# The last output block in two column halves, two late stores on another queue, one relu on another engine

## The chip, the cores and the metric

The kernel runs on one core of one Trainium2 chip. The metric is the time of one execution on the device, in microseconds (us). It is given as the median of several runs; one further execution was taken with the hardware profiler, and all views shown here come from such executions.

## The reference

The input `x` has 8 batches of 3072 rows and 256 columns. Each column is filtered along the rows by a Fourier transform, and the 24576 filtered rows then go through a small network:

```python
X = np.fft.rfft(x, axis=1)
y = np.fft.irfft(X * (filt_r + 1j * filt_i)[None], n=3072, axis=1)
t = y.reshape(24576, 256)
out = np.maximum(t @ w1, t @ w2) @ w_out      # w1, w2: 256 x 1024, w_out: 1024 x 256
```

## The kernel before

The Fourier transforms are done as matmuls with tables of sines, in stages with transposes through DRAM between them. The network is rewritten with max(a, b) = b + relu(a - b): `Wd` holds w1 - w2, `Wo` holds w_out, and `M` holds the product of w2 and w_out. So an output row is relu(t Wd) Wo + t M.

The rows are worked on in 64 tiles of 384 rows, numbered tt (eight for each batch). A tile's filtered rows lie in `yt[tt]`, its hidden values in `gt[tt]`. The loop at the end of the kernel runs over tt. In round tt it computes the hidden values of tile tt, in eight steps j of 128 hidden units (`moe_h`), and between these steps the output of tile tt - 1 (`moe_o`). A 65th round has only output matmuls left. The work of the next batch's Fourier stages is put between the steps by plans written out by hand; in the last batches little or nothing of it is left. The order of each engine's instructions is the order of the code.

In `moe_h`, step j makes one PSUM tile `ph` (L452 to L454), and relu moves it into `gt`. The table `on_v` and, from tile 8 on, the rule `j in (1, 3, 6)` say which steps VectorE does (L456); ScalarE does the others (L458).

In `moe_o`, an output tile is three blocks of 128 rows by 256 columns. Each block is a sum of ten matmuls (two with `M`, L484; eight with `Wo`, L486). Blocks are numbered q = 3 tt + c, from 0 to 191. Two blocks share one PSUM bank, and VectorE copies both at once into `ot` (L499). The last two blocks are copied on their own: block 190 by ScalarE (L490); block 191, which has a bank of its own, in two parts, columns 0 to 111 by ScalarE (L492) and columns 112 to 255 by VectorE (L493).

`out_block` issues the store of a block, 128 KB, to DRAM (L467). GpSimd issues it, but for the last two tiles (blocks 186 to 191), which SyncE issues. Each of these queues works in order: a store that waits for its copy holds up what is behind it. The pool `ps` has six PSUM buffers and `pso` has two; together they fill the eight banks.

Of the kernel before, what the change touches and what calls it, by code (L numbers as in the profile page):

```python
# [8 lines left out]
FP32 = mybir.dt.float32  # L9
BF16 = mybir.dt.bfloat16  # L10
AF = mybir.ActivationFunctionType
OP = mybir.AluOpType

B = 8
N = 3072
D = 256
# [10 lines left out]
def kernel(  # L27
# [14 lines left out]
    nc = tc.nc  # L42
    V, S, G, TE = nc.vector, nc.scalar, nc.gpsimd, nc.tensor
# [9 lines left out]
    Wo = const.tile([128, 8, D], BF16)  # L53
    M = const.tile([128, 2, D], BF16)
# [13 lines left out]
    ps = ctx.enter_context(tc.tile_pool(name="ps", bufs=6, space=bass.MemoryType.PSUM))  # L68
# [315 lines left out]

    def product(E, v, s, px, pool=None):
        pq = (pool or pqpool).tile([128, 2, 2, D], BF16, tag="pq", name="pq")
        E.tensor_tensor(pq, px.rearrange("p (o i) d -> p o i d", o=1).to_broadcast([128, 2, 2, D]),  # L387
                        F[:, :, 2 * v:2 * v + 2, s], OP.mult)
        return pq
# [36 lines left out]
    yt = {}  # L426

    def s4(tt):
        b, i = divmod(tt, 8)
        y_ = ypool.tile([128, 2, 384], BF16, tag="yt", name="y_")  # L430
        for dc in range(2):
# [11 lines left out]
    gt = {}  # L443
    on_v = {(i, j) for i in range(8) for j in range(8)
            if (j in (1, 4, 6) if 2 < 8 * i + j < 11 else j in (1, 2, 4, 6, 7) if 8 * i + j < 22
                else (j in (1, 5) and (i, j) != (3, 1)) or (i, j) == (3, 0) if 8 * i + j < 48 else j in (1, 3, 6))}

    def moe_h(tt, j):
        if j == 0:
            gt[tt] = gpool.tile([128, 8, 384], BF16, tag="gt", name="gt")  # L450
        y_ = yt[tt]
        ph = ps.tile([128, 384], FP32, tag="ps", name="ph")  # L452
        for dc in range(2):
            TE.matmul(ph, Wd[:, dc, 128 * j:128 * j + 128], y_[:, dc], start=(dc == 0), stop=(dc == 1))  # L454
        if (tt, j) in on_v if tt < 8 else j in (1, 3, 6):
            V.tensor_scalar(gt[tt][:, j], ph, 0.0, None, OP.max)  # L456
        else:
            S.activation(gt[tt][:, j], ph, AF.Relu)  # L458

    po = {}  # L460
    ot = {}

    def out_block(tt, c):
        b, i = divmod(tt, 8)
        dst = out[b * N:(b + 1) * N].rearrange("(c p i m) d -> c i p (m d)", c=3, p=32, i=8)[c, i]
        E = G if tt < 8 * B - 2 else nc.sync
        E.dma_start(out=dst, in_=ot[tt // 2][:, 3 * (tt % 2) + c])  # L467


    FIRST = ([(c, e) for c in (0, 2) for e in range(8)] + [(c, e) for c in (0, 2) for e in (8, 9)]  # L470
             + [(1, e) for e in range(10)])

    def moe_o(tt, k0, k1):
        y_, g_ = yt[tt], gt[tt]
        for k in range(k0, k1):
            c, e = divmod(k, 10) if tt else FIRST[k]
            n = e if tt else (e + 2) % 10
            q = 3 * tt + c
            blk = slice(128 * c, 128 * c + 128)
            if e == 0 and (q % 2 == 0 or q == 24 * B - 1):  # L480
                po[q // 2 % 2] = pso.tile([128, 2, D], FP32, tag="po", name="po")
            p_ = po[q // 2 % 2][:, q % 2]
            if n < 2:
                TE.matmul(p_, y_[:, n, blk], M[:, n], start=(e == 0), stop=(e == 9))  # L484
            else:
                TE.matmul(p_, g_[:, n - 2, blk], Wo[:, n - 2], start=(e == 0), stop=(e == 9))  # L486
            if e == 9 and q >= 24 * B - 2:
                e = q % 6
                if q % 2 == 0:
                    S.activation(ot[tt // 2][:, e], p_, AF.Copy)  # L490
                else:
                    S.activation(ot[tt // 2][:, e, 0:112], p_[:, 0:112], AF.Copy)  # L492
                    V.tensor_copy(ot[tt // 2][:, e, 112:D], p_[:, 112:D])  # L493
                out_block(tt, c)
            elif e == 9 and q % 2 == 1:
                if q % 6 == 1:
                    ot[tt // 2] = opool.tile([128, 6, D], FP32, tag="ot", name="ot")
                e = q % 6
                V.tensor_copy(ot[tt // 2][:, e - 1:e + 1], po[q // 2 % 2])  # L499
                for qq in (q - 1, q):  # L500
                    out_block(qq // 3, qq % 3)
# [206 lines left out]
    for tt in range(8 * B + 1):  # L708
        b, i = divmod(tt, 8)
        k = 0  # L710
        for j in range(8):
            step = 8 * i + j
            if tt < 8 * B:
                moe_h(tt, j)
            for fn, a in mid.get((b, step), ()):
                fn(*a)
            if tt > 0:
                n = 3 if j in (3, 7) else 4
                moe_o(tt - 1, k, k + n)
                k += n  # L720
            for fn, a in todo.get((b, step), ()):
                fn(*a)
            if j == (6 if i == 7 else 5 if tt == 3 else 4) and tt + 1 < 8 * B:
                s4(tt + 1)
# [30 lines left out]
```

## Time and profile before

| | |
|---|---|
| median of three runs | 501.27 us (500.65 to 502.88) |
| the profiled execution, its own time | 501.44 us |
| its span in the trace | 499.7 us |
| TensorE busy | 485.9 us (97%) |
| VectorE, ScalarE, GpSimd busy | 329.4, 309.5, 258.7 us |
| mean granted TensorE clock | 0.99 |
| last matmul ends | 494.7 us |
| last copy ends | 495.3 us |
| last store issued | 495.3 us |
| last instruction ends | 499.7 us |

Times inside the trace count from the start of its span. PE is TensorE, PEld its weight loads, DVE VectorE, ACT ScalarE, POOL GpSimd and SP SyncE; a q behind the name means its instruction queue, where stores are issued. In a line of the timeline the first number is the start, the second the length, and the bracket is the idle time of the engine before it and what ended that. The chain that ended last is followed back from the last instruction to what released it, step by step. DMA queue q1 carries what SyncE issues, q0 what GpSimd issues, and the queues called instruction carry the engines' code.

### The profile page before, as it was taken

How to read it: one execution, taken by the hardware profiler on the slowest of the kernel's cores; microseconds unless marked ns; L12 is line 12 of the kernel's file. 1: busy time of each engine (PE TensorE's matmuls, PEld its weight loads, DVE VectorE, ACT ScalarE, POOL GpSimd, SP SyncE). 2: the span in 40 equal slices, each digit the busy share in tenths (PEclk: the TensorE clock that was granted, in tenths of full speed). 3: DMA queues.
4: the chain of work that ended last, by engine and by line, in shares of the span. 5: the costliest groups of instructions: out<-in, count | busy, mean ns of one | idle time of the engine just before them, and what ended most of it. 6: DMA issues, size and time to landing. Idle time of an engine off the chain costs nothing.

```text
span 499.7 us, 13074 instructions
## 1 busy us (share of the span) xinstructions
PE 485.9 (97%) x5300; PEld 360.7 (72%) x5300; DVE 329.4 (66%) x514; ACT 309.5 (62%) x631; POOL 258.7 (52%) x342
## 2 busy tenths in 40 slices
PE   7689999999999999999999999999999999999995
PEld 3447777777777777777777777777777777777774
DVE  7876787558765678457865678457765588555552
ACT  5777488657774577647775578646776455544442
POOL 8794569339545683529446584439642211222220
PEclk9889999999999999999999999999999999999998
DMA  8999799997789668896589767895678525411112
GB/s 126 163 246 188 245 253 284 257 276 214 217 239 261 179 207 232 246 250 197 180 247 249 216 201 189 267 257 176 201 201 205 152 93 161 163 65 64 64 64 85
DMA packets 78046, 97.23 MB, mean 195 GB/s; under 512 B 8065, under 2 KB 54434, under 8 KB 77954
## 3 DMA queue, kind: packets, MB, share of 16 engines
q1 hardware_dynamic: 64786, 66.80, 50.4%
q0 software_dynamic: 13200, 29.60, 20.6%
q8 instruction: 41, 0.67, 0.6%
q14 instruction: 19, 0.16, 0.1%
HBM read 53.87 MB, written 47.19 MB: 202 GB/s over the span
## 4 chain that ended last, share of the span: by engine, by line
PE 94%; ACT 2%; DMA 2%; POOL 1%; issue 1%; DVE 0%; POOLq 0%
PE po L486 35%; PE ph L454 33%; PE po L484 8%; PE pz L405 5%; PE py L434 4%; PE px L381 2%; PE pa L354 2%; DMA xb<-in_x_dram 2%; PE pt L539 1%; PE pr L560 1%; POOL xb L88 1%; PE pa L329 1%; PE pt L533 1%; ACT bt L525 0%; PE pm__1147 L311 0%
## 5 line engine op out<-in xcount | busy, mean ns | idle before, releaser
L486 PE MATMUL po<-Wo,gt 128*128 128x256 bf16 x1536 | 261.1, 273 | 0.0
L458 ACT ACTIVATE gt<-ph 128x384 bf16<-128x384 f32 x321 | 157.8, 496 | 145.7 <-PE ph L454 144.8
L486 PEld LDWEIGHTS <-gt 128*128 128x128 bf16 x1536 | 145.9, 98 | 66.7 <-issue 12.0
L467 POOL DMA_DIRECT2D out_dram<-ot x186 | 102.9, 558 | 171.1 <-DVE ot L499 166.7
L456 DVE TENSOR_SCALAR gt<-ph 128x384 bf16<-128x384 f32 x191 | 104.5, 553 | 64.3 <-PE ph L454 60.7
L387 DVE TENSOR_TENSOR pq<-px,F 128x1024 bf16<-128x1024 f32 x91 | 106.9, 1218 | 26.2 <-PE px L381 25.9
L454 PEld LDWEIGHTS <-Wd 128*128 128x128 bf16 x1024 | 96.5, 98 | 12.5 <-issue 0.6
L103 POOL TENSOR_TENSOR xb<-XF 128x512 bf16<-128x512 f32 x48 | 61.3, 1276 | 51.4 <-DMA XF<-in_x_dram 40.4
L499 DVE COPY ot<-po 128x512 f32<-128x512 f32 x95 | 65.1, 685 | 24.8 <-PE po L486 24.8
L104 POOL TENSOR_TENSOR xb<-XF 128x512 bf16<-128x512 f32 x48 | 61.0, 1272 | 0.0
L358 ACT ACTIVATE at<-pa 128x512 bf16<-128x512 f32 x96 | 51.8, 611 | 4.2 <-PE pa L354 4.2
L409 ACT ACTIVATE zt<-pz 128x512 bf16<-128x512 f32 x84 | 45.6, 594 | 5.1 <-PE pz L405 0.8
L434 PE MATMUL py<-G,zr 96*128 96x96 bf16 x512 | 32.6, 206 | 0.1
L434 PEld LDWEIGHTS <-zr 96*128 96x128 bf16 x512 | 28.9, 97 | 2.4 <-DVE zr L563 0.6
L405 PE MATMUL pz<-pq,VP 64*64 64x256 bf16 x336 | 22.0, 281 | 0.0
L381 PE MATMUL px<-bt,U 64*64 64x256 bf16 x384 | 19.9, 278 | 1.2 <-ACT VQ L278 0.7
L405 PE MATMUL pz<-pq,VQ 64*64 64x256 bf16 x336 | 21.0, 269 | 0.0
L405 PEld LDWEIGHTS <-VP 64*64 64x64 bf16 x336 | 9.9, 105 | 13.3 <-issue 13.0
L354 PE MATMUL pa<-xb,CT 64*64 64x512 bf16 x192 | 17.6, 376 | 0.0
L381 PEld LDWEIGHTS <-U 64*64 64x64 bf16 x384 | 10.4, 108 | 3.9 <-issue 3.6
L570 PE MATMUL pd<-W 128*128 128x512 bf16 x28 | 9.7, 458 | 1.8 <-DVE zero L149 1.5
L405 PEld LDWEIGHTS <-VQ 64*64 64x64 bf16 x336 | 10.0, 106 | 0.0
(427 smaller groups left out, 603.4 us busy)
## 6 DMA issues: line engine op xcount, KB each, us to landing
out_dram<-ot POOLq DMA_DIRECT2D x186, 128.0 KB, 3.7
XF<-in_x_dram SPq DMA_DIRECT2D x96, 192.0 KB, 4.9
ad<-at SPq DMA_DIRECT2D x56, 192.0 KB, 3.7
zd<-zt SPq DMA_DIRECT2D x42, 256.0 KB, 2.8
zr<-zd SPq DMA_DIRECT2D x56, 192.0 KB, 4.8
bt<-ad SPq DMA_DIRECT2D x13, 768.0 KB, 10.7
WS<-in_moe_w_dram SPq DMA_DIRECT2D x4, 512.0 KB, 8.2
xb<-in_x_dram POOLq DMA_DIRECT2D x8, 192.0 KB, 6.2
```

What stands on the lines that cost most here:

```text
L103: G.tensor_tensor(t_[:, 0], f[:, 0], f[:, 1], OP.add)
L104: G.tensor_tensor(t_[:, 1], f[:, 0], f[:, 1], OP.subtract)
L358: S.activation(at[:, m0:m0 + 2], pa[g], AF.Copy)
L387: E.tensor_tensor(pq, px.rearrange("p (o i) d -> p o i d", o=1).to_broadcast([128, 2, 2, D]), F[:, :, 2 * v:2 * v + 2, s], OP.mult)
L405: TE.matmul(pz[g][64 * s:64 * s + 64, i], tab[64 * g:64 * g + 64, 2 * v + i, s], pq[s][64 * g:64 * g + 64, q, i], start=(q == 0), stop=(q ...
L434: TE.matmul(py[:, m], zr[b][:, 4 * i + m, 128 * dc:128 * dc + 128], G1, start=True, stop=True)
L454: TE.matmul(ph, Wd[:, dc, 128 * j:128 * j + 128], y_[:, dc], start=(dc == 0), stop=(dc == 1))
L456: V.tensor_scalar(gt[tt][:, j], ph, 0.0, None, OP.max)
L458: S.activation(gt[tt][:, j], ph, AF.Relu)
L467: E.dma_start(out=dst, in_=ot[tt // 2][:, 3 * (tt % 2) + c])
L486: TE.matmul(p_, g_[:, n - 2, blk], Wo[:, n - 2], start=(e == 0), stop=(e == 9))
L499: V.tensor_copy(ot[tt // 2][:, e - 1:e + 1], po[q // 2 % 2])
```

## The change

Block 191 is computed in two halves of 128 columns, by ten matmuls each, the first in the bank it had and the second in a tile `pl` of the pool `ps`. ScalarE copies the first half, VectorE the second. Stores 186 and 187 are issued by GpSimd instead of SyncE. The relu of tile 60, step 5, is done by VectorE instead of ScalarE.

```diff
-        if (tt, j) in on_v if tt < 8 else j in (1, 3, 6):
+        if (tt, j) in on_v if tt < 8 else j in (1, 3, 6) or (tt, j) == (8 * B - 4, 5):
             V.tensor_scalar(gt[tt][:, j], ph, 0.0, None, OP.max)
...
-        E = G if tt < 8 * B - 2 else nc.sync
+        E = G if 3 * tt + c < 24 * B - 4 else nc.sync
...
+    def last_block(tt, c, p_):
+
+        blk = slice(128 * c, 128 * c + 128)
+        for h, pp in enumerate((p_, ps.tile([128, 128], FP32, tag="ps", name="pl"))):
+            dd = slice(128 * h, 128 * h + 128)
+            for n in range(10):
+                l_, r_ = (yt[tt][:, n, blk], M[:, n, dd]) if n < 2 else (gt[tt][:, n - 2, blk], Wo[:, n - 2, dd])
+                TE.matmul(pp, l_, r_, start=(n == 0), stop=(n == 9))
+            if h == 0:
+                S.activation(ot[tt // 2][:, 3 * (tt % 2) + c, dd], pp, AF.Copy)
+            else:
+                V.tensor_copy(ot[tt // 2][:, 3 * (tt % 2) + c, dd], pp)
+        out_block(tt, c)
...
+            if q == 24 * B - 1:
+                if e == 9:
+                    last_block(tt, c, p_[:, 0:128])
+                continue
...
-            if e == 9 and q >= 24 * B - 2:
-                e = q % 6
-                if q % 2 == 0:
-                    S.activation(ot[tt // 2][:, e], p_, AF.Copy)
-                else:
-                    S.activation(ot[tt // 2][:, e, 0:112], p_[:, 0:112], AF.Copy)
-                    V.tensor_copy(ot[tt // 2][:, e, 112:D], p_[:, 112:D])
+            if e == 9 and q == 24 * B - 2:
+                S.activation(ot[tt // 2][:, q % 6], p_, AF.Copy)
                 out_block(tt, c)
```

## The prediction

> **What bounds the kernel now.** I read the page first: busy time by engine and the chain that ended last.
>
> ```profile
> PE 485.9 (97%) x5300; PEld 360.7 (72%) x5300; DVE 329.4 (66%) x514; ACT 309.5 (62%) x631; POOL 258.7 (52%) x342
> ...
> PE 94%; ACT 2%; DMA 2%; POOL 1%; issue 1%; DVE 0%; POOLq 0%
> ```
>
> TensorE carries 94% of the chain, and the change takes no arithmetic from it. So the edit can only act where TensorE is not the chain: behind its last matmul. I read that stretch next, in the chain of waits from 492.4 us to the end (start, length, what).
>
> ```profile
> 493.57 0.22 PE po L484 x2
> 493.79 0.89 PE po L486 x8
> 494.67 0.02 issue
> 494.70 0.27 ACT ot L492
> 494.97 0.02 issue
> 494.99 0.31 DVE ot L493
> ```
>
> The last block's ten matmuls take 1.11 us (0.22 + 0.89). Then ScalarE and VectorE copy their parts one after the other, although they touch different columns: 0.63 us from the last matmul to 495.30. The timeline from 494.5 us adds the store queue, SyncE (SPq):
>
> ```profile
> 494.52 1.35 SPq L467 DMA_DIRECT2D out_dram<-ot  x2
> 494.70 0.26 ACT L492 ACTIVATE ot<-po 128x112 f32<-128x112 f32 x1 [0.71 <-PE po L486]
> 494.99 0.31 DVE L493 COPY ot<-po 128x144 f32<-128x144 f32 x1 [1.79 <-ACT ot L492]
> ```
>
> The two issues under the first line lie at 494.52 to 495.06 (block 190, whose data was ready at 493.99 and waited for SyncE) and at 495.33 to 495.87 (block 191, the last). The last view is that of the stores themselves: how long each took from issue to landing (block 190 above, block 191 below), and what else the DMA engines carried from 496.8 to 497.4 us.
>
> ```profile
> DMA to landing us min/median/max: 2.0/2.0/2.0
> ...
> DMA to landing us min/median/max: 3.1/3.1/3.1
> ```
> ```profile
> q1 hardware_dynamic: 54, 0.04, 20.9%
> q14 instruction: 1, 0.01, 4.5%
> ```
>
> The last store needed 3.06 us (495.33 to 498.38) where the three before it needed 2.05 to 2.12. One packet of 8 KB of instructions starts at 496.86, amid its packets, and holds one DMA engine for 0.43 us (4.5% of 16 x 0.6 us). That engine's share of the store, eight packets, comes only after it, from 497.29 to 497.91; the other fifteen were done by 497.0. So about 1.0 us of the span is a collision of the last store with a load of code. Behind the landing are 1.3 us of closing semaphores, which the change does not touch.
>
> **The change, part by part.** The profiled execution took 501.44 us, 1.77 more than its span of 499.67; it lies 0.17 above the median of 501.27. I work out differences in the execution and apply them to the median.
>
> *Half-width matmuls.* Ten of 256 columns go, twenty of 128 come, each with its own weight load. The nearest row has this shape, 128x128 weights and 128 columns, from 42.29 us in the chain:
>
> ```profile
> 42.29 0.45 PE pt L304 x8
> ```
>
> That is 0.056 us each, so 20 x 0.056 = 1.12 against 1.11: TensorE ends at 494.68, 0.01 later. These are transposes, and a plain matmul could be slower; the upper bound is the duration of one weight load, 0.098 us (the page's weight-load rows), which gives 1.96. The lower bound is 20 x 0.043 = 0.86, from the L434 matmuls of 96 columns. I take 0.056, because its shape is the same and its weight loads, 0.098 us each, evidently overlap there.
>
> The Trainium skill, "TensorE: Matmul & The Clock Gate", section "Back-to-back issue gap", says that in a stream of weight loads and matmuls the spacing is set by both, and gives about 81 ns at 128 columns: by it the block would take 1.62 us. The row of this trace disagrees.
>
> *The copies.* Columns 0 to 127 are finished after ten half matmuls, at about 494.1; ScalarE's copy (0.264 us at 112 columns, 0.384 at 256, so 0.28) is over by 494.5 under the second half. VectorE copies the other 128 columns from another buffer: 309 ns at 144 columns and 692 at 512 give 1.04 ns a column, so 0.29 us. If it still waits for ScalarE through the tile `ot`, that wait is already over. It runs from 494.71 to 495.00 instead of ending at 495.30: 0.30 us saved.
>
> *What is late next: SyncE.* It is busy with block 190 until 495.06. Between two of its issues that wait on data stand 0.10 us (494.42 to 494.52). So block 191 cannot be issued before 495.16, and of the 0.30 only 0.17 remains.
>
> *Two stores to GpSimd.* Blocks 186 and 187 leave SyncE, where they were issued from 490.40 to 491.68. SyncE then waited for data until 493.23, so the removal starts nothing earlier. GpSimd's last work ended at 487.6; it issues both by about 491.5 (0.55 each, the page's L467 row), and they land some 2 us later, long before the end. Nothing is queued behind them. Their cover is 4.8 us (493.5 to 498.3); cost 0.
>
> *The relu.* Tile 60, j = 5 ran on ScalarE from 471.26 to 471.75. VectorE is free from 471.48 (its scaled copy L440) to 472.02, so the relu there takes 0.55 of a gap of 0.54 and pushes the next one by some 0.03. Its reader, the output matmul of the next tile, comes over 2 us later, and TensorE has no idle time there. Cost 0; without that cover it would be 0.06 (0.553 against 0.496).
>
> *The code load.* Which engine asked for it the trace does not say. Instruction counts fit VectorE: its 703 records at that moment are 128 more than the 575 at its load before, at 398.39. VectorE has one instruction more now, so the load should come a little earlier, as the store does. If the load stays at 496.86, the store, 0.17 earlier, has its packets done by 496.84 and all of 1.0 is gained. If it moves with the store, 0 is gained. If it moves 0.2 to 0.6 further ahead, the eight late packets follow it earlier and part is gained. Ends 0 and 1.0; I take 0.33, nearer to the lower end, because both events hang on the end of the same copy.
>
> The Trainium skill, "Runtime: NRT & Kernel Launch", section "Instruction fetch mechanics", calls the cost of crossing such a block mostly hidden; by it this term would be 0. The 3.1 against 2.0 above says that here it is not hidden.
>
> Sum: 0.17 + 0.33 = 0.5 us less; 501.27 - 0.5 = 500.8.
>
> **Rivals.**
>
> *Only the issue gain.* The load keeps hitting the last store in full: 501.27 - 0.17 = 501.1. For it: both move together. Against it: VectorE's extra instruction.
>
> *The load clears the store.* 0.17 + 1.0 less: 500.1. For it: 0.02 us are enough if the load stays in place, and an asked-for load that no longer hangs on the last copy would come microseconds earlier. Against it: nothing fixes its time.
>
> *Weight loads set the pace: slower.* At 0.098 us, the last matmul starts 19 x 0.098 = 1.86 us after the first (493.40), ends 0.22 later at 495.48, and VectorE is done at 495.81; the store is issued at 495.84, 0.51 late: 501.8. It decides from 0.071 us a matmul, where the copy ends at 495.30 as now. Only L304's 0.056 and L434's 0.043 speak against it. At the 81 ns of the Trainium skill ("TensorE: Matmul & The Clock Gate", "Back-to-back issue gap") the same sum gives an issue 0.19 late: 501.5.
>
> *A second code load: slower.* TensorE's own loads are larger: 41 of 16 KB on queue q8, the last at 481.38, and one fills a DMA engine for 0.96 us. They come some 250 TensorE records apart; 227 are left after the last one, and twenty more make 247. If one more falls into the last store, its 0.96 in place of 0.43 makes the store 0.5 later: 501.27 - 0.17 + 0.5 = 501.6; behind the other load on the same engine it would be 502.6.
>
> **How the numbers follow.** Forecast 0.45; only the issue gain 0.2; the load clears 0.15; weight loads 0.07; second load 0.1; 0.03 for what the trace does not show. The three runs spread from 0.6 below the median to 1.6 above. The low end is 500.1 less 0.3 of that spread, 499.8; the high end is 501.6 with 0.4, 502.0. What a measurement can tell from no change is about 0.5%, 2.5 us; no case reaches it, so nearly all lies within: 0.90. Faster by over 0.5% gets 0.06 and slower 0.04, for the remainder.
>
> **What would show it.** Right: twenty 128-column matmuls about 0.056 us apart; a single VectorE copy of 0.29 us after the last one; SyncE's last issue at about 0.17 us earlier and directly behind block 190; stores 186 and 187 on GpSimd, landed by 494. Wrong: a spacing of 0.07 or more, a last issue later than 495.33, a packet of q8 after 494, or a last store that lands in 2.05 us or in more than 3.1. A shift of the whole span ahead of 490 us would mean that I missed the mechanism.

## The result, and the profile after

The change makes the kernel slower: 503.69 us (median of 16 runs, 502.74 to 506.23) against 501.44 (16 runs). The ratio is 1.0042, with a 95% interval of 1.0029 to 1.0056: a loss of 0.4%. The profiled execution took 503.2 us, with a span of 501.4, 1.76 more than before.

The page answers to that of before line by line:

```profile
PE 485.5 (97%) x5307; PEld 361.2 (72%) x5310; DVE 329.7 (66%) x515; ACT 308.7 (62%) x630; POOL 259.6 (52%) x344
...
PE 91%; DMA 3%; DVE 2%; POOL 1%; issue 1%; ACT 0%; DVEq 0%; SPq 0%; POOLq 0%
```

TensorE is as busy as it was, and nothing here is 1.8 us longer. (Its share of the chain is lower by an early stretch in which the chain was followed through transfers instead; the last hidden matmul, L454, starts 0.26 us earlier than before, at 490.47.) The arithmetic at the end does what was said of it. The chain of waits of the changed kernel, from 493 us to the end (start, length, what):

```profile
493.31 0.56 PE po L480 x10
493.87 0.57 PE pl L480 x10
494.44 0.02 issue
494.47 0.29 DVE ot L484
```

Twenty half matmuls take 1.13 us, and one copy of 0.29 us follows instead of two in a row. The timeline from 494.2 us on has the store queue beside it:

```profile
493.65 1.89 SPq L467 DMA_DIRECT2D out_dram<-ot  x3
493.99 0.44 PE L480 MATMUL pl<-Wo,gt 128*128 128x128 bf16 x5
...
494.47 0.29 DVE L484 COPY ot<-pl 128x128 f32<-128x128 f32 x1 [1.52 <-PE pl L480]
```

VectorE no longer waits for ScalarE, and SyncE's three issues follow each other without a pause for data. The chain as the profile draws it ends here, at 494.76; the span ends at 501.4. No engine's counted work stands between. What lies there must be read elsewhere. First the last stores, from issue to landing:

```profile
DMA to landing us min/median/max: 2.0/2.1/2.1
```

(The line covers the last two stores.) The last one is issued at 495.00 and lands at 497.05, after 2.05 us instead of 3.06. So the stores too are done earlier than before. From 494 us on the DMA engines carry nothing but stores; the code packet is gone:

```profile
q1 hardware_dynamic: 576, 0.52, 18.8%
issues: line engine op xcount, KB each, median us to landing
out_dram<-ot SPq DMA_DIRECT2D x3, 128.0 KB, 2.1
```

The waits of SyncE's queue from 494 us on show the rest (who, for whom, us in total, times, longest):

```profile
SPq L763 <- PEq L763: 4.1, 2, 3.6
SPq L763 <- DMA out_dram<-ot: 1.0, 2, 0.6
```

and before:

```profile
SPq L750 <- DMA out_dram<-ot: 2.4, 2, 1.8
SPq L750 <- PEq L750: 0.7, 2, 0.5
```

The first line of after has grown from 0.7 to 4.1 us, the second has shrunk from 2.4 to 1.0. SyncE waits once for 3.6 us in the closing part of the program (L763 is the launch line, where the end of the kernel is booked). TensorE is named, but its own closing drain had ended at 494.48, so it cannot be what SyncE waited for. What the launch line's instructions did on each engine shows who was late. GpSimd (POOLq) has three closing DRAIN instructions there. After (duration in ns, min/median/max, then first and last start):

```profile
L763 POOLq DRAIN  x3: 51/106/9800, 490.8 to 501.2; - x3
```

and before, where the launch line is L750:

```profile
L750 POOLq DRAIN  x3: 51/106/9640, 487.0 to 499.4; - x3
```

The first of them is GpSimd's first closing instruction, and it lasts 9.64 us before and 9.80 us after. It stands right behind GpSimd's last store and ends 9.0 to 9.1 us after that store's issue ends. Before, it ran from 486.96 to 496.60, and SyncE's own closing drains were through at 498.90: 2.3 us of slack. After, it runs from 490.83 to 500.63, because GpSimd's last work is later. GpSimd's last two stores after:

```profile
490.41 1.09 POOL L467 DMA_DIRECT2D out_dram<-ot  x2 [3.04 <-DVE ot L512]
```

and before:

```profile
486.53 1.09 POOL L467 DMA_DIRECT2D out_dram<-ot  x2 [3.06 <-DVE ot L499]
```

In the kernel after, these are stores 186 and 187. The landing of stores is not what ends the drain: GpSimd's last store lands at 489.07 before and at 492.92 after, more than 7 us before the drain ends. SyncE is through at 497.19 and waits for GpSimd; 0.8 us of semaphores follow the drain, and the program ends at 501.43.

### The profile page after: what moved, and what is told of

Read it like the earlier page. It is cut to its first block, busy times and chain, and to the rows that moved or that the text cites. A ratio compares the mean times of both kernels' runs of the same rounds, so it can differ in the third digit from the quotient of the medians.

```text
span 501.4 us, 13091 instructions
## 1 busy us (share of the span) xinstructions
PE 485.5 (97%) x5307; PEld 361.2 (72%) x5310; DVE 329.7 (66%) x515; ACT 308.7 (62%) x630; POOL 259.6 (52%) x344
## 4 chain that ended last, share of the span: by engine, by line
PE 91%; DMA 3%; DVE 2%; POOL 1%; issue 1%; ACT 0%; DVEq 0%; SPq 0%; POOLq 0%
PE po L504 34%; PE ph L454 33%; PE po L502 8%; PE pz L405 5%; PE py L434 4%; PE pa L354 2%; PE px L381 2%; DMA xb<-in_x_dram 2%; DVE pq L387 1%; PE pr L573 1%; POOL xb L88 1%; DMA zr<-zd 1%; DMA F<-in_filt_r_dram 1%; PE pa L329 1%; POOL F L121 1%
## 5 line engine op out<-in xcount | busy, mean ns | idle before, releaser
L454 PEld LDWEIGHTS <-Wd 128*128 128x128 bf16 x1024 | 96.5, 98 | 12.5 <-issue 0.6
```

## The experiments

Theory D was that GpSimd's drain, put off by the two stores, sets the end. Its rival H was that the halves make the end late and that the drain only shows it. Theory L concerned the load of code that hit the last store before. Each experiment names its base kernel in the expectation.

**The change without its two GpSimd stores** (e1).

```diff
-        E = G if 3 * tt + c < 24 * B - 4 else nc.sync
+        E = G if tt < 8 * B - 2 else nc.sync
```

> The change without its two GpSimd stores: all of the last six stores stay on SyncE; halves and relu as in the change. Theory D (GpSimd's closing drain ends about 9.1 us after the issue of its last store, and with stores 186 and 187 that is after everything else): GpSimd's last store is issued by 487.4 again, the drain ends at about 496.4, and the closing semaphores run right behind SyncE's drain at 497.2, as early as the profile of the change shows it. The end is then 497.2 + 0.8 = 498.0 in the trace, 3.4 before the change and 1.4 to 1.7 before the kernel before: about 499.9. Rival H (the halves make the closing part late, and GpSimd's drain only shows it): the end stays near 501.4 in the trace, about 503.5.

Measured: 500.61 us against 501.42, ratio 0.9984 (0.9973 to 0.9995); the span of the profiled execution, whose time was 500.02, is 498.2. GpSimd's drain in the launch line's view:

```profile
L763 POOLq DRAIN  x3: 51/106/9637, 486.7 to 498.0; - x3
```

It starts at 486.7 again and ends at 496.33, before SyncE is through at 497.47. So the halves and the relu together are a gain, and H falls.

**The two stores alone** (e2).

```diff
-        E = G if tt < 8 * B - 2 else nc.sync
+        E = G if 3 * tt + c < 24 * B - 4 else nc.sync
```

> The kernel before with stores 186 and 187 issued by GpSimd, and nothing else. Theory D: their issue ends at about 491.75, the drain at about 490.8 + 10.1 = 500.9, the end 0.8 later at 501.7, 2.0 after the kernel before: about 503.4, although the last store lands before 498.5. Rival H: no halves, so no loss: 501.4.

Measured: 503.46 against 501.42, ratio 1.0042 (1.0030 to 1.0054), the whole loss of the change. The same two views of it:

```profile
L750 POOLq DRAIN  x3: 51/102/9803, 490.7 to 501.0; - x3
```
```profile
SPq L750 <- PEq L750: 3.0, 2, 2.5
```

The last store of this kernel lands 3.1 us after its issue, as in the kernel before, and that no longer matters: SyncE is through at 498.22 and waits 2.5 us for the drain.

**The relu alone** (e3).

```diff
-        if (tt, j) in on_v if tt < 8 else j in (1, 3, 6):
+        if (tt, j) in on_v if tt < 8 else j in (1, 3, 6) or (tt, j) == (8 * B - 4, 5):
```

> The kernel before with the relu of tile 60, step 5, on VectorE, and nothing else. Theory L (the code load that hit the last store belongs to VectorE and comes when VectorE has gone a fixed number of instructions; one more instruction lets it come some 7 us earlier, as in the profile of the change): no 8 KB packet after 494, the last store lands in 2.05 us instead of 3.06, the end is 1.0 earlier: about 500.4. Rival: the relu alters nothing, the load stays near 496.9 and the time at 501.4.

Measured: 500.74 against 501.42, ratio 0.9990 (0.9980 to 0.9999). The last store's landing, and the DMA queues from 494 to 498 us, where before a q14 packet had stood:

```profile
DMA to landing us min/median/max: 2.0/2.0/2.0
```
```profile
q1 hardware_dynamic: 576, 0.52, 37.5%
issues: line engine op xcount, KB each, median us to landing
out_dram<-ot SPq DMA_DIRECT2D x4, 128.0 KB, 2.1
```

The 8 KB packet has gone to 489.93, where no last store is in flight.

**The halves alone** (e4): e1 without the relu's move.

```diff
-        if (tt, j) in on_v if tt < 8 else j in (1, 3, 6) or (tt, j) == (8 * B - 4, 5):
+        if (tt, j) in on_v if tt < 8 else j in (1, 3, 6):
```

> The kernel before with the last block in two halves, and nothing else. VectorE has as many instructions as before. Theory L: the load stays behind the last copy and comes at about 496.5, in or just after the packets of the last store; the store is issued 0.2 earlier and lands in 2.1 to 3.1 us: between 500.2 and 501.3, nearest to 501.2. Rival (the twenty half matmuls or the removed ScalarE wait move the load): no packet of code after 494, 500.2. Theory D adds nothing here, since GpSimd's last store is that of before.

Measured: 501.11 against 501.42, ratio 0.9993 (0.9984 to 1.0001), not told apart from no change. The packet is still late, at 495.63, and the last store lands in between:

```profile
DMA to landing us min/median/max: 2.7/2.7/2.7
```

So the halves by themselves leave the collision in place; it is the relu that removes it.

**Four stores on GpSimd instead of two** (e5).

```diff
-        E = G if 3 * tt + c < 24 * B - 4 else nc.sync
+        E = G if 3 * tt + c < 24 * B - 2 else nc.sync
```

> The change with two more stores on GpSimd, 188 and 189; SyncE keeps only 190 and 191. Theory D: GpSimd's last issue moves from 491.5 to about 494.1 (both wait for the copy that ends at 492.95), the drain ends some 9.1 us after it at 503.2, and the end of the trace is near 504.0, 2.6 after that of the change: about 506.2. Rival (GpSimd's drain ends at a fixed place that has to do with the end of the other engines, not with its own last store): the end stays near 501.4, about 503.6.

Measured: 506.67 against 501.49, ratio 1.0097 (1.0082 to 1.0112). The drain and SyncE's wait:

```profile
L763 POOLq DRAIN  x3: 51/106/9963, 494.0 to 504.5; - x3
```
```profile
SPq L763 <- PEq L763: 7.1, 2, 6.6
```

GpSimd's last issue ends at 494.70 instead of 491.50, the drain at 504.00 instead of 500.63. The end follows GpSimd's last store, and not the other engines, which were through at 497.56.

**A late GpSimd copy in place of late stores** (e6), on e1.

```diff
+                if q == 24 * B - 5:
+                    G.tensor_copy(CT[:, 0, :], ot[tt // 2][:, e, 0:64])
```

> The run with halves and relu and no late GpSimd stores, plus one small GpSimd copy (128 x 64 into a table that nothing reads any more) that waits for the same VectorE copy as stores 186 and 187 and so runs at about 490.2 to 490.6. Theory D1 (the long drain follows GpSimd's stores alone): the drain still ends about 9.0 us after the last store's issue, at 496.4, and nothing changes: 500.6. Theory D2 (it follows any late work of GpSimd): the drain ends at about 499.6, the end is near 500.4 in the trace: about 502.8.

Measured: 502.17 against 501.49, ratio 1.0009 (0.9999 to 1.0019), not told apart from the kernel before; beside e1's 500.61 it is 1.6 later, with a span of 499.7 against 498.2. The copy ends at 489.89, the drain at 498.88:

```profile
489.65 0.24 POOL L516 CAST CT<-ot 128x64 bf16<-128x64 f32 x1 [2.81 <-DVE ot L512]
```
```profile
L765 POOLq DRAIN  x3: 51/102/9247, 489.6 to 499.4; - x3
```

So D2 holds: a late copy of 0.24 us puts the drain off as the stores did. The last work need not be a store.

**One more VectorE instruction** (e7), on the kernel before.

```diff
     V.memset(zero, 0.0)
+    V.memset(zero, 0.0)
```

> The kernel before with one tiny VectorE memset doubled in the setup, and no other edit: VectorE has one instruction more, and no relu moves. Theory L (the place of VectorE's code load is set by its count of instructions): the load comes near 490 instead of 496.9, the last store lands in 2.05 us, and the time is that of the run with the relu alone: about 500.7. Rival (it was the moved relu itself): the load stays near 496.9, the store lands in about 3 us: 501.4.

Measured: 500.39 against 501.49, ratio 0.9977 (0.9967 to 0.9987). The packet of code comes at 489.55, and the last store lands after:

```profile
DMA to landing us min/median/max: 2.0/2.0/2.0
```

A useless instruction of the setup does what the moved relu did. So the relu's share of the gain comes from the one instruction more on VectorE and not from where the relu runs. ScalarE has one instruction fewer in e3 but not here, so its count is not needed for the effect.

**Store 190 issued by ScalarE** (e8), on e1.

```diff
+            if h == 0:
+                out_block(tt, c - 1, S)
```

(`out_block` takes the engine as an argument, and block 190's own call is taken out.)

> The run with halves and relu and no late GpSimd stores, with store 190 issued by ScalarE after its half copy, so that SyncE is free for store 191 when VectorE's copy ends. If SyncE's issue of 190 is what holds up 191, the last issue comes at about 494.78 instead of 494.92 and the end 0.14 earlier: about 500.5 beside 500.6. If the end is set by the closing semaphores of SyncE in their order instead, nothing or up to 0.4 either way.

Measured: 500.36 against 501.49, ratio 0.9968 (0.9946 to 0.9990). Counted from the last hidden matmul, the last issue comes 0.10 us earlier than in e1 (4.35 against 4.45). The two versions are not told apart by their times; by the intervals, each is faster than the kernel before, by 0.2 to 0.3%.

**The last eight tiles' stores on SyncE** (e9), on e1.

```diff
-        E = G if tt < 8 * B - 2 else nc.sync
+        E = G if tt < 8 * B - 8 else nc.sync
```

> The run with halves and relu, with the stores of the last eight tiles (24 instead of 6) issued by SyncE; GpSimd's last store is then issued at about 462. Theory D: the drain begins there and is over before 472, and the end of the trace, which SyncE's closing part sets, is that of the run with six stores on SyncE, about 498.2: 500.6. What it tells besides is the drain's length: about 9.0 us if it is fixed, about 7.5 if it grows with the number of stores issued by GpSimd (8.97, 9.13 and 9.30 us were seen with 186, 188 and 190 stores, 0.08 a store, and 18 are taken away). Rival: an in-order queue with 24 stores on SyncE delays the reads that stand in it, and the time rises.

Measured: 500.60 against 501.10, ratio 0.9988 (0.9973 to 1.0002), not told apart from no change; no gain beside e1, since the drain was already hidden there. GpSimd's last store is issued at 450.1, earlier than the 462 that I had named: tile 55 is done by then. The drain is shorter:

```profile
L763 POOLq DRAIN  x3: 51/106/8167, 450.0 to 498.6; - x3
```

**Every second tile's stores on SyncE** (e10), on e1.

```diff
-        E = G if tt < 8 * B - 2 else nc.sync
+        E = G if tt < 8 * B - 2 and tt % 2 == 0 else nc.sync
```

> The run with halves and relu, with the stores of every odd tile issued by SyncE from the start: GpSimd issues 93 stores instead of 186, its last one at about 482.4. One look at the drain's length. If it grows by 0.08 us with each store that GpSimd has issued in the whole run, it is 8.97 - 93 x 0.0817 = 1.4 us long. If it depends on when it begins, or has a floor, it is 8 to 9 us. The time itself can go either way, since SyncE's queue also holds the reads and stores of the Fourier stages in order; it says nothing on the two theories.

A single run took 502.75 us beside 500.18 of the kernel before; one run each gives no verdict. The drain:

```profile
L763 POOLq DRAIN  x3: 51/106/3053, 485.1 to 500.7; - x3
```

It ends 2.48 us after the last issue: far from 8 to 9, and longer than the straight line's 1.4. All drains together:

| kernel | stores by GpSimd | its last work ends | drain ends | difference | SyncE through | span |
|---|---|---|---|---|---|---|
| before | 186 | 487.63 | 496.60 | 8.97 | 498.90 | 499.67 |
| e1 | 186 | 487.36 | 496.33 | 8.97 | 497.47 | 498.25 |
| e6 | 186, a copy | 489.89 | 498.88 | 8.99 | 496.95 | 499.67 |
| the change | 188 | 491.50 | 500.63 | 9.13 | 497.19 | 501.43 |
| e2 | 188 | 491.40 | 500.54 | 9.13 | 498.22 | 501.33 |
| e5 | 190 | 494.70 | 504.00 | 9.30 | 497.56 | 504.79 |
| e9 | 168 | 450.70 | 458.20 | 7.50 | 498.06 | 498.83 |
| e10 | 93 | 485.69 | 488.17 | 2.48 | 500.20 | 500.98 |

In all rows the program ends 0.8 us after the later of drain and SyncE. The drain is longer where GpSimd issued more stores, and the time at which it begins does not set its length: e10's begins 1.8 us ahead of that of before, and what is left of it behind GpSimd's last work is little more than a quarter. It does not grow in a straight line: 0.08 us a store from 168 to 190 stores, 0.07 from 93 to 168. In e10 the late stores are thinner too (its last 19 take 76.8 us from first to last issue, those of before 37.3), so it alone does not tell whether the whole run's number counts or that of late stores. e9 speaks for the whole run: its last 19 take 38.8 us, nearly as before, and its drain is 1.5 us shorter. What the drain does in these microseconds was not seen.

## Why the prediction was wrong

*The step that failed is "Two stores to GpSimd".* It said that nothing is queued behind the two stores and put their cost at 0, under a cover of 4.8 us reckoned from their landing. Something is queued behind them: the closing drain, on the same in-order queue. It was in the trace before, in the view of the launch line, which the prediction did not read. For the same reason it was wrong that the change does not touch the closing part: behind the last landing stand 4.4 us (497.05 to 501.43) in place of 1.3. The cover that mattered was the slack of that drain, 498.90 - 496.60 = 2.3 us, and GpSimd's last issue moved by 491.50 - 487.63 = 3.87. With the prediction's own 491.5 for that issue, the trace before would have given 496.60 + 3.87 + 0.8 = 501.3; the drain was also 0.16 longer, and the measured span is 501.43. The term is 3.2 us (501.43 against e1's 498.25) in place of 0. It is larger than 3.87 - 2.3 because the halves and the relu bring SyncE through earlier, at 497.47 in e1, and so leave the drain a slack of only 1.1 us.

*Half-width matmuls: right.* 0.056 us each was taken from the transposes, and the kernel's own row gives 0.56 for ten. The 81 ns that the Trainium skill ("TensorE: Matmul & The Clock Gate", "Back-to-back issue gap") gives for such a stream do not occur here either. The rival of weight loads as the bound falls with it.

*Copies and SyncE: the mechanism right, the size off.* SyncE does issue store 191 behind store 190 and not when the copy ends: 494.76 against 495.00 in the change. Counted from the last hidden matmul, the last issue is 0.15 us earlier in e1 and in e4, near the 0.17 of the sum, but only 0.07 in the change. There SyncE's first two issues after a long pause, 188 and 189, took 0.635 and 0.603 us, and the third 0.601; in e1, where 186 and 187 come first, those three took 0.538, 0.613 and 0.546. So taking two stores off SyncE was not free on its own queue either.

*The code load: mis-sized.* I took 0.33 of the 1.0 us and gave 0.15 to a load that clears the store. It cleared the store in full: 3.06 us became 2.05, because the packet moved from 496.86 to 489.67. I had expected a shift of parts of a microsecond from one more VectorE instruction, although the rival "The load clears the store" named the other case; e3 and e7 show that one is enough for 7 us. All nine kernels here that have that instruction show the early load, and the three without it (before, e2, e4) the late one. Why it jumps so far is open: the load came at VectorE's 703rd record before and at its 700th after, so a bare count does not explain it. The Trainium skill, "Runtime: NRT & Kernel Launch", "Instruction fetch mechanics", calls the cost of crossing a 16 KiB boundary in an engine's code mostly hidden. The cost here is another one, to a store whose packets stand behind the load of 8 KB: e4 and e7, with 2.7 and 2.0 us for the same store, show that it depends on where the load falls. No second load came, and that rival falls. Its count could not have decided: in the trace before, TensorE's loads lie 161 to 407 of its records apart.

*The relu: cost 0 holds.* No loss shows in e3, which has the move alone; one of 0.06 us could not be told apart there.

*The sum.* e1's span is 1.43 less than before. Of that, 0.26 was there already at the last hidden matmul, whose start varies from 489.95 to 491.05 us in the traces of e1 to e8 and which I do not count as the change's making; 0.15 is the issue and 1.02 the landing. By the medians the gain is 0.8 (0.3 to 1.4 by the interval); the profiled execution of e1 is 0.6 faster than its median. The prediction's 0.5 less lies in that interval, but this agreement is in part luck, since 0.33 stood where the trace shows 1.02. The whole change gained nothing from it, because the end hung on the drain: the change and e2, with and without halves and relu, are at 503.69 and 503.46.

Neither of the two slower rivals had this mechanism: both looked for the loss ahead of the last landing, and it lies behind it. So 503.69 lies above the range, whose high end, 502.0, came from the second code load.

## What to carry to other kernels

Before giving late work to an engine, look at what the end of the program makes that engine do: find each engine's closing drain in the trace and compare its end with that of the last store's landing. The chain of busy work does not show it, and SyncE's wait may be booked on another engine that was long done. When a store's landing is much longer than that of its neighbours, look for a packet of code among its packets before looking for a cause in the store.

## What the runs showed of the hardware

GpSimd's closing drain took 7.5 to 9.3 us after its last work with 168 to 190 stores issued by it and 2.5 us with 93, and a late copy of 0.24 us put it off as stores did. The landing of GpSimd's stores did not end it: in the kernel before, the last of them landed 7.5 us ahead of the drain's end. In the three traces with an 8 KB packet of code at 495.6 to 496.9 us (before, e2, e4) the last store landed in 2.7 to 3.1 us; in the nine others, where it came between 488.9 and 492.4, ahead of the last store's issue, it landed in 2.0 to 2.1. One more instruction on VectorE decided between the two.
